# Second half's products of ones moved ahead of the first tile's products, its root ahead of a weight join, and two chunk pairs' loads held until that root is made

## The chip, the cores and the metric

The kernel runs on one core of one Trainium2 chip. The metric is the device time in microseconds of one execution, lower is better. The kernel before takes 598.52 us in the median of three runs.

## What is computed

Three stages follow each other on 4 x 768 = 3072 tokens of 256 numbers: a chunked linear recurrence with decay (8 heads, 32 wide, state 16), a gated network of width 1536 behind an RMS norm, and a second gated network of width 2048. All of it is float32.

```python
def _attn_ref(x, a, B, C):
    ...
    for c in range(nc):
        ...
        L = np.exp(cum[:, :, :, None] - cum[:, :, None, :]) * causal
        CB = np.einsum('bhin,bhjn->bhij', Cc, Bc)
        y_intra = np.einsum('bhij,bhjd->bhid', CB * L, xc)
        y_inter = np.einsum('bhin,bhnd->bhid', Cc, state) * decay_to_i[:, :, :, None]
        ...
        state = decay_full[:, :, None, None] * state + np.sum(Bx, axis=2)

def _moe_ref(x, w_gate, w_val, w_out, rms_g):
    rms = np.sqrt(np.mean(x * x, axis=-1, keepdims=True) + 1e-06)
    xn = x / rms * rms_g
    g = xn @ w_gate
    silu = g * (1.0 / (1.0 + np.exp(-g)))
    return silu * (xn @ w_val) @ w_out

def _moe2_ref(x, w_in, w_out):
    h = x @ w_in
    g = h * np.clip(h + 3.0, 0.0, 6.0) / 6.0
    return g @ w_out
```

## The kernel before

**Work items.** The recurrence works on 24 chunks (number k), two at a time: a pair of chunks has the number q = k // 2. Chunks 0 to 3 (pairs 0 and 1) belong to the first 128 positions of the four batches; their 512 tokens are the first token tile (j = 0) of the first network. Pairs 2 and 3 are the next 512 tokens, and so on. The network's weights come as 12 tiles f = 0 to 11 of 768 columns; each tile is loaded by SyncE's queue (`yT<-w`, `rawx<-w`), converted by ScalarE (`wa`, `wb`: lines 831 and 835), joined by VectorE (`wj`, line 839), and split into a high part (`wh`, a CAST at line 292 or 294) and a low part (`wl`, a TENSOR_TENSOR at line 288), which are both called `w1t` in the profile. A product of the network is three passes: high x high, low x high, high x low.

**Order.** `P.op` records each operation with an estimated cost, what it reads and writes; `Plan.run` places them on the engines in the order of a simulated schedule, and `P.chain` fixes the order of named operations on one engine by hand. So the order is decided when the program is built; on the chip each engine runs its list in order and waits on semaphores. The schedule of GpSimd (POOL) holds the DMAs of the chunk pairs from pair 2 on: `L` (the decays, spread over 64 partitions), `cb` (B, C and x of the pair) and `P` (the decay products).

**The opening.** For the first tile the norm is done in two halves of two chunks (`norm_pair`, q = 0 and 1). For the second half, the steps are:

- `sq2`, `sq3` (ScalarE, line 637): squares of the recurrence's output; `mn2`, `mn3` (TensorE, line 658): products with a column of ones, which sum them;
- `rt1` (ScalarE, line 695): square root; `v1`, `iv1`, `nw1` (VectorE, lines 691, 699, 678 to 680): mean, reciprocal, one Newton step;
- `bk1` (TensorE, line 703): spreads the factor; `sx10`, `sx11` (VectorE, line 708): scale x; `xh10`, `xh11` (ScalarE) and `xl1` (VectorE): split x into high and low.

The first products of the network, `h000`, `h001`, `h100`, `h101` (weight tile, half, gate or value), use the first half; `h010` and those after it use the second half. Between the visit `visit1` and `h010` the plan puts idle products of zeros (`idle`, line 389, about 0.43 us each, written to `acc` or `sps`) where it sees TensorE waiting. Behind `h010` the plan's own order goes on: the products of tiles f = 2, 3, ..., the visits of the chunk pairs, the norm of the next token tile.

The calls for the second half's loads stand at line 495 and after (`ld_L`, `ld_cb2`, `ld_P`); a weight load that writes the same buffers as an earlier one waits for its readers. Chunk pair 2 and pair 3 each load two `L` of 256 KB, a `cb` of 896 KB and two `P` of 64 KB.

Of the kernel before, what the change touches and what calls it, by code (L numbers as in the profile page):

```python
# [16 lines left out]
B, H, S, D, N = 4, 8, 768, 32, 16  # L17
CH = 128
SC = 64
# [200 lines left out]
def block_kernel(ctx, tc, comb, ablk, a1st, w1, w2d, cst, out):  # L220
    nc = tc.nc
    pe, act, dve, pool = nc.tensor, nc.scalar, nc.vector, nc.gpsimd
# [32 lines left out]
    P = Plan({"L": 2, "cb": 2, "P": 2, "ch": 4, "bh": 2, "SM": 4, "um": 4, "V": 6, "V1": 4,  # L255
              "Sc": 1, "Su": 1, "Sy": 1, "Ss": 1, "xT": 1, "sq": 1, "rn": 1, "rb": 1, "x": 2, "p": 3, "gh": 3,
              "gl": 3, "raw": NRAW, "tmp": 3, "raw2": 1, "s2": 2, "st": 1, "h": 2, "hb": 4, "acc": 2})
# [7 lines left out]
    def dma(nbytes, n=1, e="DMA"):  # L265
        return {e: max(560 * n, nbytes // 370) if e == "DMA" else (1000 if e == "POOL" else 560) * n,
                "bytes": nbytes}
# [54 lines left out]
    pref = dram.tile([NK, H * CH], F32, name="pref")  # L322
# [57 lines left out]
    def tile2(n, q, shape):  # L380
        if (n + "2", q) not in T:
            t = T[n + "2", q] = ap2.tile([128, 2] + shape, F32, tag=n, name=n)
            for i in range(2):
                T[n, 2 * q + i] = t[:, i]
        return T[n + "2", q]
# [60 lines left out]
    def load(q):  # L446
        k0, bst = 2 * q, BOOST if 2 * q >= B else BOOST0
# [21 lines left out]
                pool.dma_start(out=t[:, i], in_=src.to_broadcast([H, N, CH]))  # L469

        cbs, Ls = [("cb", q, i) for i in range(2)], [("L", q, i) for i in range(2)]
        seq = [("raw", 3)] if q == B // 2 else []
        if q == 0:
            P.op(dma(8192, 1, "ACT"), lambda e: act.dma_start(
                out=ac[:32, 4], in_=a1st),
                w=[("ac", 1)], boost=2e6)
            P.op(dma(400000), lambda e: nc.sync.dma_start(out=ac[:, :4], in_=rows(ablk)),
                 w=[("ac", 0)], boost=1e6)
            P.op(dma(33792, 1, "ACT"), lambda e: act.dma_start(out=gs, in_=cst), w=[("cs", 0)],
                 boost=75e4)  # L480
            P.op({"ACT": 1500}, lambda e: act.activation(out=spare, in_=half, func=AF.Sqrt),
                 w=[("table", 0)], boost=5e5)
            prefixes()
            broadcast()
        if q < B // 2:
            for i, e in enumerate(("ACT", "DMA")):
                P.op(dma(458752, 1, e), lambda e, i=i: ld_cb(e, i), w=[cbs[i]],
                     boost=8e5 - 1e5 * q)
        if q == B:
            def hold(e):  # L490
                t = tile2("L", q, [H, SC])
                pool.tensor_copy(t[:, 0, 0, :1], T["sq", 1][:, 0, NT // NB - 1:NT // NB])

            P.op({"POOL": 200}, hold, r=[("sq", 1, B - 1)], w=Ls, boost=bst)
        if q >= B // 2:
            P.op(dma(1048576, 2, "POOL"), ld_L, r=[("azero", 0)], w=Ls, boost=bst, seq=seq)
            P.op(dma(917504, 1, "POOL"), ld_cb2, w=cbs, boost=bst, seq=seq)
            P.op(dma(262144, 2, "POOL"), ld_P, r=[("pref", 0), ("pref", 1)], w=[("P", q)], boost=bst)


        def scan(e, k):
# [16 lines left out]
        for i, k in enumerate((k0, k0 + 1)):  # L518
            P.op({"DVE": ds(512)}, lambda e, k=k: scan(e, k),
                 r=[("eye8", 0), Ls[i] if k >= B else ("Lp", k)], w=[Ls[i]], boost=bst,  # L520
                 seq=[("x", 0, 1, 2)] if q == B // 2 else [], tag=f"scan{k}")
# [3 lines left out]
                 w=[("ch", k)], boost=bst, tag=f"ch{k}")  # L525
# [55 lines left out]
    def back_keys(k):  # L581
        r = [("SM", k), ("cb", k // 2, k % 2), ("V1", k), ("ch", k)]
        return r + ([("V", k - B)] if k >= B else []), [("Sy", k // 2, k % 2)]
# [77 lines left out]
    def rn(j):  # L661
        if ("rn", j) not in T:
            T["rn", j] = [ap1.tile([128, B], F32, tag=n, name=n) for n in ("v0", "y0", "z0")]
        return T["rn", j]
# [177 lines left out]
    def weights(f, cols, src, raw, tmp, wh, wl, bst=0, soon=0, seq=(), hold=()):  # L842
# [28 lines left out]
        if hold:  # L871
            P.op({"POOL": 200}, lambda e: hold[0](raw(f)), r=hold[1], w=[kr], boost=soon, seq=seq)
        P.op(dma(size), load, w=[kr], boost=soon, seq=seq)
        if wide:
            P.op({"ACT": a1(cols)}, high, r=[kr], w=[kt], boost=bst, tag=f"wa{f}")
# [152 lines left out]
    def first(ks):  # L1028
        intra(ks)
        inter(ks, 1)  # L1030

    load(0)
    for q in range(2):
        ks = [2 * q, 2 * q + 1]
        for k in ks:
            rf, wf = front_keys(k)
            P.op({"PE": 350}, lambda e, k=k: score(k), r=rf[:1] + [("open0", 0)][:q], w=wf[:1],
                 boost=BOOST0 + 3000, ps=q, tag=f"sc{k}")
        for k in ks:
            rf, wf = front_keys(k)  # L1040
            P.op({"PE": 250}, lambda e, k=k: grow(k), r=rf, w=wf[1:], boost=BOOST0 + 3000,
                 seq=[("Sc", q, 1)], ps=q, tag=f"gr{k}")
        if q == 0:
            spread[0]()
            load(1)
            P.op({"HOST": 0}, open0, r=[("L", n, i) for n in range(2) for i in range(2)] +
                 [("P", n) for n in range(2)] + [("z", 0)], w=[("open0", 0)])
    for q in range(2):
        ks, r, w = [2 * q, 2 * q + 1], [], []
        for k in ks:  # L1050
            middle(k)
            r, w = r + back_keys(k)[0], w + back_keys(k)[1]
# [4 lines left out]
         w=[("open", 1)])  # L1057
    P.op({"ACT": 1500}, lambda e: act.activation(out=spare, in_=half, func=AF.Silu),
         r=[("rn", 0, q, 2) for q in range(2)], w=[("table", 0)], boost=1e6,
# [4 lines left out]
    def hold(f):  # L1064
        def go(t):
            pool.tensor_copy(t[:, :1], T["cb", 3][:, :1])

        return (go, [("cb", 1, 1)]) if f == 3 else ()

    for f in range(F1):  # L1070
        weights(f, 768, w1, raw1,
                lambda f: yflat[:, 4608 + f % 3 * 768:][:, :768] if f % 3 < 2 else extra, w1h, w1l,
                bst=(W0 - 2000 * f if f < 2 else 0), soon=1e5 if f < 2 else 0,
                seq=[("azero", 0)] + ([("raw", 3)] if f > 3 else []), hold=hold(f))
# [35 lines left out]
    for j in range(NJ):  # L1110
        acc = [nxt(nacc), nxt(nacc)]
        for f in range(F1):
# [14 lines left out]
            if n == NB - 1:  # L1127
                P.op({"HOST": 0}, open2, r=[("yT", i, t) for i in range(NJ * B, NK) for t in range(2)],
                     w=[("open", 2), ("open", 0)] + [("un", n) for n in range(NU)])
# [334 lines left out]
    while pending:  # L1464
# [1 line left out]
        pending.pop(0)[1]()  # L1466
    P.chain("PE", order)
    P.chain("DVE", "spot0 spot1 spot2 spot3 clip each prefix scan0 bh0 scan1 bh1 ch0 ch1 SM0 SM1 um0 "
            "um1 scan2 scan3 bh2 bh3 ch2 ch3 wj0 v0 iv0 nw0 SM2 SM3 um2 um3 sx00 sx01 wl0 xl0 wj1 wj2 "
            "v1 iv1 nw1 wl1 sx10 sx11 xl1")  # L1470
    P.chain("ACT", "P0 P1 wa0 wb0 sq0 sq1 wa1 rt0 ev0 ev1 wh0 wb1 wa2 xh00 xh01 sq2 sq3 wb2 wh1 rt1 ev2 "
            "ev3 silu xh10 xh11")
    P.chain("PE", "heat sp0 sp1 sc0 sc1 px gr0 gr1 sp2 sp3 visit0 zero mn0 mn1 sc2 sc3 gr2 gr3 bk0 warm visit1 "
            "h000 mn2 mn3 h001 bk1 h100 h101")
    P.fill = idle, 430, "visit1", "h010"
    with tc.manual_schedule():
        setup()
# [59 lines left out]
```

## Time and profile before

| what | us or share |
|---|---|
| median of three runs (lowest, highest) | 598.52 (597.91, 599.05) |
| profiled execution | 598.91 |
| its span in the trace | 596.8 |
| TensorE busy, share of the span | 587.6, 98% |
| VectorE busy | 475.2, 80% |
| ScalarE busy | 369.3, 62% |
| GpSimd busy | 34.9, 6% |
| DMA issues: `w` tiles of 768 KB (page, 6) | 4.7 to 10.4 us to landing |
| instruction queue q8 (page, 3) | 34 packets, 0.56 MB |

The profiled execution lies 0.39 us above the median. Of its 598.91 us, 2.1 lie outside the span. A busy time is a sum over the whole span, in which the stages have different limits. The granted TensorE clock is at its upper level (2.4 GHz) from 5.7 us on, the whole stretch that this text speaks of.

### The profile page before, as it was taken

The page shows a single profiled execution, that of the slowest core. Times are in us where ns is not written, and L with a number is a line of the kernel's source. Part 1 is how long each engine was busy: PE and PEld are TensorE (multiplying, and loading weights), DVE is VectorE, ACT ScalarE, POOL GpSimd, SP SyncE. Part 2 cuts the span into 40 slices and gives each one's busy share as a digit, 9 for nine tenths or more (in the row PEclk, how much of TensorE's full clock was granted, in tenths as well). Part 3 has the DMA queues.
Part 4 walks back from the last instruction along what each step waited for, and adds up shares of the span by engine and source line. Part 5 has one row for each costly group of instructions (what it writes and reads, how often), then busy time and mean ns, then how long its engine had stood idle before and what let it go on. Part 6 is the DMA issues. An engine that isn't in the chain of part 4 may idle for free.

```text
span 596.8 us, 10877 instructions
## 1 busy us (share of the span) xinstructions
PE 587.6 (98%) x4356; PEld 474.8 (80%) x4356; DVE 475.2 (80%) x911; ACT 369.3 (62%) x649; POOL 34.9 (6%) x63
## 2 busy tenths in 40 slices
PE   9899999999999999999999999999999999999997
PEld 6787888788778778877787878888888888888885
DVE  8899977947886588799998898887975759765665
ACT  3889523333433354676766788787876758776663
POOL 3202013102220000000000000000000000000000
PEclk9999999999999999999999999999999999999999
DMA  8994205304340010122010102100000000100001
GB/s 332 340 322 151 65 18 153 115 11 125 123 154 20 22 68 23 49 71 70 1 70 2 70 2 70 71 1 1 36 36 1 0 2 0 72 0 1 0 1 71
DMA packets 11131, 40.91 MB, mean 69 GB/s; under 512 B 2484, under 2 KB 3208, under 8 KB 10056
## 3 DMA queue, kind: packets, MB, share of 16 engines
q1 hardware_dynamic: 6312, 23.25, 10.9%
q0 software_dynamic: 4000, 15.74, 8.5%
q10 hardware_dynamic: 768, 1.22, 0.6%
q8 instruction: 34, 0.56, 0.4%
q14 instruction: 17, 0.14, 0.1%
HBM read 36.84 MB, written 3.35 MB: 67 GB/s over the span
## 4 chain that ended last, share of the span: by engine, by line
PE 89%; DVE 7%; ACT 1%; issue 1%; DMA 1%; DVEq 0%; ACTq 0%; SPq 0%
PE hps L917 59%; PE acc L917 24%; PE sps L562 1%; DVE st L288 1%; DVE unit L288 1%; PE sps L536 1%; PE sps L572 1%; DMA raw<-w 1%; DVE gl L288 1%; PE spread L396 1%; PE sps L547 1%; DVE p L288 1%; DVE w1t L288 0%; DVE L L505 0%; PE acc L389 0%
## 5 line engine op out<-in xcount | busy, mean ns | idle before, releaser
L917 PE MATMUL hps<-xh,w1t 128*128 128x512 f32 (+1 forms) x544 | 146.2, 387 | 1.0 <-ACT p L946 0.8
L917 PEld LDWEIGHTS hps<-xh,w1t 128*128 128x128 f32 x544 | 99.5, 188 | 23.2 <-ACT p L946 1.3
L917 PE MATMUL hps<-xl,w1t 128*128 128x512 f32 (+1 forms) x380 | 108.8, 385 | 0.0
L917 PE MATMUL hps<-unit,w1t 128*128 128x512 f32 x324 | 90.2, 389 | 0.0
L917 PE MATMUL acc<-gh,w1t 128*128 128x512 f32 (+1 forms) x288 | 88.0, 387 | 0.0
L917 PEld LDWEIGHTS hps<-xl,w1t 128*128 128x128 f32 x380 | 70.8, 188 | 14.5
L917 PEld LDWEIGHTS hps<-unit,w1t 128*128 128x128 f32 x324 | 60.8, 188 | 12.7
L288 DVE TENSOR_TENSOR gl<-p,gh 128x512 fp32r<-128x512 f32 (+1 forms) x86 | 57.5, 674 | 14.2 <-ACT gh L954 8.0
L917 PEld LDWEIGHTS acc<-gh,w1t 128*128 128x128 f32 x288 | 53.0, 188 | 11.3 <-issue 0.6
L954 ACT CAST gh<-p 128x512 fp32r<-128x512 f32 (+1 forms) x50 | 30.2, 606 | 50.7 <-PE acc L917 50.0
L917 PE MATMUL acc<-gl,w1t 128*128 128x512 f32 (+1 forms) x158 | 60.7, 384 | 0.0
L1261 ACT ACTIVATE p<-hps,half 128x512 f32<-128x512 f32 x48 | 33.0, 688 | 34.1 <-PE hps L917 34.1
L288 DVE TENSOR_TENSOR unit<-hps,unit 128x512 f32<-128x512 f32 x36 | 24.8, 689 | 36.3 <-PE hps L917 36.2
L950 DVE TENSOR_TENSOR p<-p,hps 128x512 f32<-128x512 f32 (+1 forms) x50 | 33.1, 663 | 24.8 <-PE hps L917 21.7
L946 ACT ACTIVATE p<-hps 128x512 f32<-128x512 f32 (+1 forms) x50 | 28.9, 581 | 37.1 <-DVE gl L288 19.2
L917 PE MATMUL acc<-unit,w1t 128*128 128x512 f32 x142 | 42.8, 389 | 0.0
L1264 DVE SCALAR_TENSOR_TENSOR p<-p,hps 128x512 f32<-128x512 f32 x48 | 33.0, 687 | 10.7 <-ACT p L1261 10.5
L1261 ACT ACTIVATE p<-unit,half 128x512 f32<-128x512 f32 x48 | 34.7, 722 | 1.1 <-DVE unit L288 0.7
L1268 ACT CAST unit<-p 128x512 fp32r<-128x512 f32 x48 | 29.7, 621 | 8.9 <-DVE p L1264 7.4
L917 PEld LDWEIGHTS acc<-gl,w1t 128*128 128x128 f32 x158 | 29.7, 188 | 6.2
L1268 ACT CAST gh<-p 128x512 fp32r<-128x512 f32 x48 | 29.5, 619 | 7.2 <-DVE p L1264 6.4
L1264 DVE SCALAR_TENSOR_TENSOR p<-p,unit 128x512 f32<-128x512 f32 x48 | 33.1, 689 | 0.8 <-ACT p L1261 0.4
(181 smaller groups left out, 967.2 us busy)
## 6 DMA issues: line engine op xcount, KB each, us to landing
cb<-comb POOLq DMA_DIRECT2D x10, 896.0 KB, 5.1
raw<-w SPq DMA_DIRECT2D x8, 1024.0 KB, 4.7
L<-azero POOLq DMA_DIRECT2D x20, 256.0 KB, 4.1
yT<-w SPq DMA_DIRECT2D x6, 768.0 KB, 9.9
rawx<-w SPq DMA_DIRECT2D x6, 768.0 KB, 10.4
out<-yT SPq DMA_DIRECT2D x10, 256.0 KB, 2.1
P<-pref POOLq DMA_DIRECT2D x20, 64.0 KB, 2.5
rb<-rnd SPq DMA_DIRECT2D x5, 256.0 KB, 3.0
```

Of the source, the lines that this page charges most:

```text
L288: eng[e].tensor_tensor(out=out, in0=a, in1=b, op=op)
L396: pe.matmul(out=Q[3][:, :128 * n], lhsT=nc.const_aps.tensor(0.0, [128, 128]), rhs=nc.const_aps.tensor(0.0, [128, 128 * n]), start=True, st ...
L536: pe.matmul(out=o[64 * c:64 * c + 64, p ^ c], lhsT=cb[r, BN + c * SC:BN + (c + 1) * SC], rhs=cb[r, CP + c * CH:CP + (c + 1) * CH], start=T ...
L547: m = pe.matmul(out=o[32 * p:32 * p + 32, c], lhsT=b[r, s:s + 32], rhs=cb[r, XX + 64 * p:XX + 64 * p + 64], start=False, stop=True, skip_g ...
L562: pe.matmul(out=part(k, Y)[32 * g:32 * g + 32, 2 * t + c], rhs=T["SM", k][r, h ^ 2 * c], lhsT=T["cb", k][r, XX + D * h:XX + D * h + D], st ...
L917: pe.matmul(out=o, lhsT=a, rhs=c, start=first and i == 0, stop=last and i == len(seq) - 1, skip_group_check=skip)
L946: act.activation(out=p[:, :n], in_=hcols(0), func=AF.Silu)
L950: dve.tensor_tensor(out=p, in0=p, in1=hcols(1), op=ALU.mult)
L954: act.copy(out=t[:, :n], in_=T["p", i][:, :n])
L1261: act.activation(out=unit(pk), in_=h(), func=AF.Relu, scale=1.0 / 6.0, bias=half)
L1264: dve.scalar_tensor_tensor(out=unit(pk), in0=unit(pk), scalar=1.0, in1=h(), op0=ALU.min, op1=ALU.mult)
L1268: P.op({"ACT": a1(512) + 20}, lambda e: act.copy(out=unit(gk), in_=unit(pk)), r=[pk], w=[gk])
```

## The change

Three things are edited. In the hand-written chains, TensorE now has `mn2 mn3` ahead of `h000` and `bk1` ahead of `h001`; ScalarE has `rt1 ev2 ev3` ahead of `wh1`; VectorE has `v1 iv1 nw1` ahead of `wj2`, and `wl1` behind `sx10 sx11`. GpSimd copies one column of `y` (the second half's factor) into the `L` tile of pair 2 ahead of that pair's loads, so that they cannot start before the factor is there; `cb` and `P` of the pair are ordered behind this copy, and pair 3's loads behind pair 2's `L`. The plan then makes a new order of what follows.

```diff
-        seq = [("raw", 3)] if q == B // 2 else []
+        seq = [("raw", 3)] if q == B // 2 else [("L", 2, 0)] if q == 3 else []
...
+        if q == B // 2:
+            def hold(e):
+                t = tile2("L", q, [H, SC])
+                pool.tensor_copy(t[:, 0, 0, :1], rn(0)[1][:, 2:3])
+
+            P.op({"POOL": 200}, hold, r=[("rn", 0, 1, 1)], w=Ls + [("hold", 0)], boost=bst, seq=seq)
+            seq = [("hold", 0)]
         if q >= B // 2:
             P.op(dma(1048576, 2, "POOL"), ld_L, r=[("azero", 0)], w=Ls, boost=bst, seq=seq)
             P.op(dma(917504, 1, "POOL"), ld_cb2, w=cbs, boost=bst, seq=seq)
-            P.op(dma(262144, 2, "POOL"), ld_P, r=[("pref", 0), ("pref", 1)], w=[("P", q)], boost=bst)
+            P.op(dma(262144, 2, "POOL"), ld_P, r=[("pref", 0), ("pref", 1)], w=[("P", q)], boost=bst, seq=seq)
...
     P.chain("DVE", "spot0 spot1 spot2 spot3 clip each prefix scan0 bh0 scan1 bh1 ch0 ch1 SM0 SM1 um0 "
-            "um1 scan2 scan3 bh2 bh3 ch2 ch3 wj0 v0 iv0 nw0 SM2 SM3 um2 um3 sx00 sx01 wl0 xl0 wj1 wj2 "
-            "v1 iv1 nw1 wl1 sx10 sx11 xl1")
-    P.chain("ACT", "P0 P1 wa0 wb0 sq0 sq1 wa1 rt0 ev0 ev1 wh0 wb1 wa2 xh00 xh01 sq2 sq3 wb2 wh1 rt1 ev2 "
-            "ev3 silu xh10 xh11")
+            "um1 scan2 scan3 bh2 bh3 ch2 ch3 wj0 v0 iv0 nw0 SM2 SM3 um2 um3 sx00 sx01 wl0 xl0 wj1 "
+            "v1 iv1 nw1 wj2 sx10 sx11 wl1 xl1")
+    P.chain("ACT", "P0 P1 wa0 wb0 sq0 sq1 wa1 rt0 ev0 ev1 wh0 wb1 wa2 xh00 xh01 sq2 sq3 wb2 rt1 ev2 ev3 "
+            "wh1 silu xh10 xh11")
     P.chain("PE", "heat sp0 sp1 sc0 sc1 px gr0 gr1 sp2 sp3 visit0 zero mn0 mn1 sc2 sc3 gr2 gr3 bk0 warm visit1 "
-            "h000 mn2 mn3 h001 bk1 h100 h101")
+            "mn2 mn3 h000 bk1 h001 h100 h101")
```

The new lines move the line numbers behind line 495 by 7. On TensorE, behind `visit1` (the last row of `ch,um`), the kernel before has one idle product into `sps`, two into `acc`, `h000` (six rows of `hps`), the four products of ones, `h001`, three idle products and `bk1` (`eye,y`):

```order
L572 MATMUL sps<-ch,um 64x64 x8
L389 MATMUL sps_107<-zero 128x256
L389 MATMUL acc<-zero 128x256 x2
L917 MATMUL hps<-xh,w1t_68 128x256 x4
L917 MATMUL hps<-xl,w1t_68 128x256 x2
L658 MATMUL sps<-ones,sq 128x1 x4
L917 MATMUL hps<-xh,w1t_68 128x256 x4
L917 MATMUL hps<-xl,w1t_68 128x256 x2
L389 MATMUL acc<-zero 128x256 x3
L703 MATMUL sps<-eye,y_317 128x128 x2
```

The changed kernel has at the same place:

```order
L579 MATMUL sps<-ch,um 64x64 x8
L389 MATMUL sps_107<-zero 128x256
L389 MATMUL acc<-zero 128x256
L665 MATMUL sps<-ones,sq 128x1 x4
L924 MATMUL hps<-xh,w1t_68 128x256 x4
L924 MATMUL hps<-xl,w1t_68 128x256 x2
L389 MATMUL acc<-zero 128x256 x3
L710 MATMUL sps<-eye,y_312 128x128 x2
L924 MATMUL hps<-xh,w1t_68 128x256 x4
L924 MATMUL hps<-xl,w1t_68 128x256 x2
L389 MATMUL acc<-zero 128x256 x2
```

The products of ones stand ahead of `h000`, with one idle product fewer before them; `bk1` stands ahead of `h001`; the three idle products that stood ahead of `h010` have become two ahead of `h100`. On VectorE, from the join `wj1` on, the kernel before has `wj2` (`fold`), a high part of tile 2, the second half's factor, `wl1`, `sx10 sx11`, `wl2` and `xl1`:

```order
L839 SCALAR_TENSOR_TENSOR yT<-yT 128x768
L839 SCALAR_TENSOR_TENSOR fold<-fold,yT 128x768
L294 CAST w1t_69<-fold 128x768
L691 TENSOR_SCALAR v_316<-sps 128x2
L699 RECIPROCAL y_317<-z_318 128x2
L680 SCALAR_TENSOR_TENSOR y_317<-z_318,y_317 128x2
L288 TENSOR_TENSOR w1t_68<-yT,w1t_68 128x768
L708 SCALAR_TENSOR_TENSOR xT<-xT,gs,sps 128x256 x2
L288 TENSOR_TENSOR w1t_69<-fold,w1t_69 128x768
L288 TENSOR_TENSOR xl<-xT,xh 128x2x256
```

The changed kernel has there:

```order
L846 SCALAR_TENSOR_TENSOR yT<-yT 128x768
L698 TENSOR_SCALAR v_311<-sps 128x2
L706 RECIPROCAL y_312<-z_313 128x2
L687 SCALAR_TENSOR_TENSOR y_312<-z_313,y_312 128x2
L846 SCALAR_TENSOR_TENSOR fold<-fold,yT 128x768
L294 CAST w1t_69<-fold 128x768
L715 SCALAR_TENSOR_TENSOR xT<-xT,gs,sps 128x256 x2
L288 TENSOR_TENSOR w1t_68<-yT,w1t_68 128x768
L288 TENSOR_TENSOR xl<-xT,xh 128x2x256
L957 TENSOR_TENSOR p<-p,hps 128x256
L288 TENSOR_TENSOR w1t_69<-fold,w1t_69 128x768
```

The factor stands ahead of `wj2`, `wl1` (`w1t_68`) behind `sx10 sx11`, and `wl2` (`w1t_69`) has moved behind `xl1` and the first gated product `p`. On POOL, the kernel before issues the first loads of pairs 2 and 3 in this order, behind a copy that belongs to the weights:

```order
L1066 COPY rawx_104<-cb 128x1
L454 DMA cb<-comb 128x2x896
L460 DMA L<-azero 64x1024 x2
L469 DMA P<-pref 128x1x128 x2
L460 DMA L<-azero 64x1024 x2
L454 DMA cb<-comb 128x2x896
L469 DMA P<-pref 128x1x128 x2
```

The changed kernel issues them in this one:

```order
L1073 COPY rawx_104<-cb 128x1
L498 COPY L<-y_312 128x1
L460 DMA L<-azero 64x1024 x2
L454 DMA cb<-comb 128x2x896
L469 DMA P<-pref 128x1x128 x2
L460 DMA L<-azero 64x1024 x2
L454 DMA cb<-comb 128x2x896
L469 DMA P<-pref 128x1x128 x2
```

All ten stand behind the new copy, and pair 2's `cb` behind its `L`. Further down on VectorE, the scans of pair 3 (`L<-L`, some 20 rows behind the piece above) stand in the difference of the two programs so, - before and + changed:

```order
 L288 TENSOR_TENSOR gl<-p,gh 128x256
-L505 SCALAR_TENSOR_TENSOR L<-L,eye_101 128x512
 L288 TENSOR_TENSOR w1t_70<-fold,w1t_70 128x768
-L505 SCALAR_TENSOR_TENSOR L<-L,eye_101 128x512
-L593 TENSOR_TENSOR SM<-sps,L 128x512
-L600 TENSOR_TENSOR um<-sps,gs 128x128
-L593 TENSOR_TENSOR SM<-sps,L 128x512
-L600 TENSOR_TENSOR um<-sps,gs 128x128
+L512 SCALAR_TENSOR_TENSOR L<-L,eye_101 128x512 x2
```

The first of them has moved behind a low part of a weight tile. The first scan of pair 2 likewise has one gated product `p` more ahead of it.

## Rows read from the trace of the kernel before

**Rows 1.** Windows: stretch, its length, busy us (count) of PE, PEld, DVE, ACT, POOL, clock, DMA share, GB/s.
```profile
20.00:29.00 9.00, 8.03 (x53) 7.29 (x53) 7.34 (x17) 7.18 (x15) 1.51 (x3) 1.00 1.03 296
29.00:57.70 28.70, 28.70 (x458) 23.78 (x459) 28.38 (x52) 24.88 (x42) 4.11 (x7) 1.00 0.71 236
69.60:590.00 520.40, 518.09 (x3447) 420.09 (x3446) 408.11 (x767) 318.19 (x560) 20.91 (x34) 1.00 0.13 42
```
**Rows 2.** Timeline of PE: start, us, line, operation, tiles, count [idle before <-releaser].
```profile
20.01 1.13 PE L389 MATMUL acc<-zero 128*128 128x256 f32 x4
20.79 0.83 PE L917 MATMUL hps<-xh,w1t 128*128 128x256 f32 x4
...
21.69 0.39 PE L658 MATMUL sps<-ones,sq 128*128 128x1 f32 x3
22.92 0.61 PE L658 MATMUL sps<-ones,sq 128*128 128x1 f32 x5 [0.84 <-issue]
23.39 0.72 PE L917 MATMUL hps<-xh,w1t 128*128 128x256 f32 x4
...
24.19 1.46 PE L389 MATMUL acc<-zero 128*128 128x256 f32 x6
25.48 0.61 PE L703 MATMUL sps<-eye,y 128*128 128x128 f32 x4
```
**Rows 3.** Timeline of DVE, 20 to 29 us.
```profile
20.58 0.95 DVE L839 SCALAR_TENSOR_TENSOR yT<-yT 128x768 int32<-128x768 int32 x1
...
23.86 0.16 DVE L691 TENSOR_SCALAR v<-sps 128x2 f32<-128x2 f32 x1 [0.86 <-ACT z L695]
...
24.60 0.95 DVE L288 TENSOR_TENSOR w1t<-yT,w1t 128x768 fp32r<-128x768 f32 x1
26.20 0.87 DVE L708 SCALAR_TENSOR_TENSOR xT<-xT,gs,sps 128x256 f32<-128x256 f32 x2 [0.66 <-PE sps L703]
27.00 0.95 DVE L288 TENSOR_TENSOR w1t<-fold,w1t 128x768 fp32r<-128x768 f32 x1
27.87 0.68 DVE L288 TENSOR_TENSOR xl<-xT,xh 128x512 fp32r<-128x512 f32 x1
```
**Rows 4.** Timeline of ACT, 21 to 28 us.
```profile
21.57 0.83 ACT L292 CAST w1t<-yT 128x768 fp32r<-128x768 f32 x1 [0.56 <-DVE yT L839]
23.57 0.26 ACT L695 ACTIVATE z<-sps,eps 128x2 f32<-128x2 f32 x1 [1.16 <-PE sps L658]
...
26.72 0.80 ACT L292 CAST xh<-xT 128x256 fp32r<-128x256 f32 x2
```
**Rows 5.** Timeline of DVE, 30 to 58 us.
```profile
30.67 1.22 DVE L505 TENSOR_TENSOR_SCAN L<-L,eye 128x512 f32<-128x512 f32 x1
...
39.34 1.22 DVE L505 TENSOR_TENSOR_SCAN L<-L,eye 128x512 f32<-128x512 f32 x1
40.48 0.93 DVE L288 TENSOR_TENSOR w1t<-fold,w1t 128x768 fp32r<-128x768 f32 x1
...
44.24 0.29 DVE L288 TENSOR_TENSOR bh<-cb,L 128x128 f32<-128x128 f32 x1
...
55.38 0.69 DVE L950 TENSOR_TENSOR p<-p,hps 128x512 f32<-128x512 f32 x1 [0.32 <-ACT w1t L292]
```
**Rows 6.** Timeline of POOL: the later hold of the kernel before.
```profile
54.50 0.60 POOL L492 COPY L<-sq 128x1 f32<-128x1 f32 x1
```
**Rows 7.** DMA queues from 23 to 27 us: packets, MB, share of 16 engines.
```profile
q1 hardware_dynamic: 140, 0.76, 68.4%
q0 software_dynamic: 140, 0.35, 35.9%
```
**Rows 8.** The same from 17.5 to 20 us, the POOL queue, while a cb moves.
```profile
q0 software_dynamic: 88, 0.63, 60.6%
```
**Rows 9.** DMA issue at 47.98 us: KB, us to landing.
```profile
cb<-comb POOLq DMA_DIRECT2D x1, 896.0 KB, 4.9
```
**Rows 10.** Tile L, four loads issued from 13.6 to 18.5 us.
```profile
DMA to landing us min/median/max: 12.2/14.5/16.5
```

## The prediction

> **What bounds the kernel now.** The windows come first [rows 1]. From 69.6 to 590 us TensorE is busy 518.09 of 520.40 us: nothing there waits, and the edits do not reach it. From 29 to 57.7 us TensorE is busy all 28.70 us, and VectorE 28.38 of them: two full engines, of which VectorE has a single idle of 0.32 us (at 55.38, behind a high part of a weight tile) [rows 5]. Only from 20 to 29 us is there room: TensorE 8.03 of 9.00 us, and part of that is idle products of zeros; VectorE 7.34. In the same window the DMA engines show a busy share of 1.03: every transfer there delays another.
>
> Then the timelines, engine by engine. On TensorE, `h000` starts at 20.79 and lasts 0.90, the products of ones start at 21.69, stand still for 0.84 us in the middle of the row (behind nothing that the profile shows), and are through at 23.39 [rows 2]. ScalarE, done with `wh1`, waits 1.16 us for them and takes the root at 23.57 [rows 4]; VectorE idles 0.86 us for the root, does the factor from 23.86 to 24.60, then `wl1`, idles 0.66 for `bk1`, and starts `sx10` at 26.20, `wl2` at 27.00, `xl1` at 27.87 [rows 3]. `h010` needs `xl1`, and idle products (two right ahead of `h000`, three right ahead of `bk1`) fill TensorE's gaps until then. So the second half's factor is a chain of waits worth about 1.5 us of VectorE's idle time, but VectorE, not TensorE, carries the debt afterwards.
>
> What reaches the end? Behind 57.7 us comes the next token tile's norm, a chain that VectorE begins, and behind it TensorE's full stretch from 69.6 [rows 1]. With VectorE 99% busy up to that norm, I count the gain that lasts by VectorE's shift, not by TensorE's.
>
> **The early part, term by term.** TensorE: one idle product fewer (1.29 us for three, from 24.19 to 25.48, is 0.43 each [rows 2]), so the ones start at 20.01 + 0.43 = 20.44 in place of 21.69. Without the stall the row takes 23.39 - 21.69 - 0.84 = 0.86: through at 21.30. Before, the root started 0.18 behind that end and the first step of the factor 0.29 behind the root's start [rows 2 to 4]: root 21.48, factor 21.77 to 22.51. TensorE: `h000` until 21.30 + 0.90 = 22.20, three idle products until 23.49, `bk1`; `sx10` came 0.72 behind `bk1`: 24.21, 1.99 earlier. VectorE is free for it: from 22.51 `wj2` 0.95 [rows 3] and the CAST (at most the 0.83 of ScalarE's CAST of that size [rows 4]) end by 24.29. Then `sx10 sx11` 0.80, `wl1` 0.87 (the distance to the next start), so `xl1` could go at 25.96. ScalarE ends later: root 21.48, then 3.15 to `xh10` (the distance from 23.57 to 26.72), plus `wh1` 0.83, which now stands behind the root, and 0.80 for `xh10` and `xh11` [rows 4]: 26.26. So `xl1` starts at 26.3 instead of 27.87: 1.6 earlier for `h010` and TensorE.
>
> VectorE's own account is smaller: `wl2` (0.87), done ahead of `xl1` before, is now behind the first `p`. The shift on VectorE is 1.57 - 0.87 = **0.70 us**. Two idle products fewer on TensorE cost nothing, since they only fill.
>
> Whether the 0.84 stall goes is not shown by any row. No semaphore ends it. It stands inside eight products of one form, beside DMA engines at a share of 1.03, and what TensorE has to be given there is its instructions. If it is that, it hangs on the DMA load at that time, and the hold takes POOL's 3 MB away from exactly there; I take it as gone. If it stays, 0.84 is lost from both accounts: 0.73 on TensorE, 0.14 lost on VectorE. The Trainium skill ("Runtime: NRT & Kernel Launch", section "Instruction fetch mechanics") says that engines refetch their program in blocks of 256 instructions and that a crossing is mostly hidden. By that, the stall would not be a fetch and would stay; the row, 0.84 us idle with no releaser [rows 2], fits an unhidden one better.
>
> **The hold, and what queues behind it.** POOL's copy waits for the factor at 22.51; it takes 0.60, as the later hold of the same form does [rows 6]: the first `L` is issued at 23.1. Before, the first `L` was issued at 13.6 and the fourth at 18.5 [rows 10], and `cb` before both. Behind the copy on POOL stand only the ten loads, all in order: two `L`, `cb`, two `P`, two `L`, `cb`, two `P`. The consumers that come first are VectorE's scans, and behind each scan stands all of VectorE's later work: high and low parts, gated products. Pair 2's first scan ran at 30.67; 0.70 earlier, and one `p` (some 0.4) more ahead of it, makes 30.4. Pair 3's first ran at 39.34; 0.70 earlier, but now behind a low part of 0.93 [rows 5], makes 39.6.
>
> When do the `L` land? In a stretch shared with weights, POOL's queue moved 0.35 MB in 4 us, 87 GB/s, while it held `L` and `P` [rows 7]; with `cb` moving it did 0.63 MB in 2.5 us, 252 GB/s [rows 8]. A `cb` alone, 4.9 us to landing [rows 9], is 3.6 us of bytes at that rate and 1.3 us of start. So first bytes at 23.1 + 1.3 = 24.4; pair 2's two `L`, 0.52 MB, take 6.0: 30.4, just in time. Up to pair 3's second `L` there are 1.05 MB of `L`, 0.92 of `cb` and 0.13 of `P`: 12.0 + 3.6 + 1.5 = 17.1 us, landing at 41.5 if every `L` moves beside weights, a wait of 1.9. The lower bound is everything at 252 GB/s, 8.3 us, 32.7, no wait anywhere. The upper bounds are the lags of before [rows 10], though a `cb` and its 3.6 us stood ahead of those: 23.1 + 12.2 = 35.3 for pair 2's, a wait of 4.9; for pair 3's, with the issues spread over 4.9 us as before, 28.0 + 16.5 = 44.5, a wait of 4.9 too. The two don't add up, since who has waited once is later at the other place. I take **1.0 us**, between none and 1.9: the weights run alone until 24.4 and should leave gaps later (the share from 29 to 57.7 is 0.71 on the mean [rows 1]), but under load a start is hardly shorter than that of the lone `cb`. Pair 3's `cb` follows its `L` within 3.6, 41.5 - 0.9 + 3.6 = 44.2 with that wait, and `bh`, at 44.24 before [rows 5], is due at 44.24 - 0.70 + 1.0 = 44.5: nothing more.
>
> The Trainium skill ("DMA: Bandwidth & Descriptors", section "Queues, rings and completion order") says that each DMA engine takes turns between its queues packet by packet. The row agrees: 140 packets of either queue in 4 us [rows 7]. By that rule the small packets of `L` get no more than half the turns as long as weights are queued, the stream lands at 41.5, the wait is 1.9 and the sum below becomes +0.9: it speaks against holding the loads.
>
> **Sum.** VectorE: -0.70 (early part) + 1.0 (wait for `L`) = +0.3, which the idle of 0.32 at 55.38 takes up: 0.0. The profiled execution stays at 598.9, which lies 0.39 above the median, so on the scale of the median 598.5. What a measurement of this kernel can tell from no change is about 0.2%, 1.2 us: the forecast is no visible difference.
>
> **Rivals.**
> 1. *The loads land later still*, with the lag of before: a wait of 2.5 to 4.9, less 0.70 and 0.32, makes +1.5 to +3.9: 600.0 to 602.4. For it: the share of 1.03, equal packet counts, the lags of 12.2 to 16.5 [rows 1, 7, 10]. Against: no `cb` is ahead of pair 2's `L` any more, and the weights will have run ahead. It decides from a wait of 2.2 on, a landing of pair 2's `L` at 32.6 or of pair 3's at 41.8.
> 2. *The loads are in time and the early gain arrives.* Without a wait VectorE keeps 0.70: 597.8, still within 0.2%. If TensorE's 1.6 lasts as well, because the debt of `wl2` goes into idle time, 598.5 - 1.2 to 1.6: 596.9 to 597.3, faster. Against: VectorE's 28.38 of 28.70, with almost no idle to pay from [rows 1].
> 3. *The stall stays with the products of ones*, so the edits to the chains do next to nothing: early part +0.14 in place of -0.70, the hold ends 0.84 later, the scans are due 0.84 later, so the same wait: 0.14 + 1.0 - 0.32 = +0.8, 599.3, at the edge of slower.
> 4. *A new stall of TensorE's instructions* while the held loads move, 0.84 again [rows 2]: taken up where VectorE is the bound, since TensorE is ahead by 1.6. It changes no number unless it is longer.
>
> **Chances.** The forecast (a wait of 0 to 2, VectorE's gain alone): 0.47. Rival 1: 0.25. Rival 2's faster end: 0.16. The stall that stays: 0.12, a third of it beyond 0.2%. So faster 0.16, slower 0.25 + 0.04 = 0.29, same 0.55. The range leaves at most 0.2 outside: low 597.0, inside the faster case; high 601.0, a wait of 3.5, short of the upper bounds, which need the whole lag of before although less is queued ahead.
>
> **What would show it.** In the changed kernel: ones from about 20.4 in one piece (or again with an idle behind nothing), `bk1` at 23.5, `sx10` at 24.2, `xl1` at 26.3, `h010` behind it. If `xl1` isn't ahead of 27, the early part is wrong; its likeliest failure is ScalarE, with `wh1` now behind the root. The copy on POOL near 22.5, the first `L` issued near 23.1; then the landings of the second and the fourth `L`, and VectorE's idle ahead of the scans of pairs 2 and 3, with those transfers as its end. No idle there and a time below 597.3: rival 2. An idle of 2.5 or more: rival 1. Wrong altogether I would be if a wait opened elsewhere, above all on TensorE between 29 and 57.7 us, where before there was none, or if the weights, which move alone while POOL's loads are held, had been what the opening waited for.

## The result and the profile after

| what | before | changed |
|---|---|---|
| median, five executions each (lowest, highest) | 598.66 (597.91, 599.05) | 603.12 (602.69, 603.57) |
| ratio, 95% interval | | 1.0077 (1.0065, 1.0089) |
| profiled execution, its span | 598.91, 596.8 | 603.12, 601.0 |
| TensorE, VectorE, ScalarE, GpSimd busy | 587.6, 475.2, 369.3, 34.9 | 589.1, 475.2, 369.4, 35.7 |
| mean granted clock of TensorE in the executions | 0.999 in the profiled one | 0.996 to 0.997 |

The changed kernel is 4.5 us (0.77%) slower. The forecast was no visible difference (598.5) in a range from 597.0 to 601.0; the measured time lies above it, on the side of rival 1. TensorE is busy 1.5 us longer although it has two idle products fewer. That is the first hint that something beyond a wait happened. Of the kernel before, one execution of 2048.65 us is left out in all that follows.

The windows of the changed kernel (columns as in [rows 1]):

```profile
29.00:33.40 4.40, 3.57 (x25) 2.97 (x23) 1.84 (x5) 4.11 (x9) 0.69 (x2) 1.00 1.01 241
33.40:34.90 1.50, 0.00 (x0) 0.00 (x0) 1.50 (x3) 0.65 (x1) 0.60 (x1) 1.00 1.07 287
...
36.00:37.00 1.00, 1.00 (x4) 0.71 (x3) 0.63 (x1) 0.34 (x1) 0.00 (x0) 0.50 1.05 227
37.00:38.00 1.00, 1.00 (x4) 0.81 (x3) 0.76 (x2) 1.00 (x2) 0.00 (x0) 0.50 0.96 267
38.00:39.00 1.00, 1.00 (x4) 0.79 (x3) 1.00 (x2) 0.33 (x1) 0.00 (x0) 0.50 1.09 294
...
40.00:44.00 4.00, 4.00 (x47) 3.46 (x53) 3.73 (x8) 3.50 (x7) 0.00 (x0) 1.00 1.01 316
```

Where [rows 1] showed TensorE busy all 28.70 us, it now stands still, with nothing at all from 33.4 to 34.9, and then runs at 0.50 of its clock, that is at 1.2 GHz, in every window from 36 to 39. VectorE's timeline says why (its rows answer to [rows 3, 5]):

```profile
21.86 0.16 DVE L698 TENSOR_SCALAR v<-sps 128x2 f32<-128x2 f32 x1 [0.29 <-ACT z L702]
...
25.05 0.87 DVE L715 SCALAR_TENSOR_TENSOR xT<-xT,gs,sps 128x256 f32<-128x256 f32 x2 [0.81 <-PE sps L710]
25.84 0.95 DVE L288 TENSOR_TENSOR w1t<-yT,w1t 128x768 fp32r<-128x768 f32 x1
26.71 0.68 DVE L288 TENSOR_TENSOR xl<-xT,xh 128x512 fp32r<-128x512 f32 x1
...
33.35 1.23 DVE L512 TENSOR_TENSOR_SCAN L<-L,eye 128x512 f32<-128x512 f32 x1 [2.56 <-DMA L<-azero]
...
43.60 2.33 DVE L512 TENSOR_TENSOR_SCAN L<-L,eye 128x512 f32<-128x512 f32 x2
```

The first scan of pair 2 was ready to go at 33.35 - 2.56 = 30.79 and waited 2.56 us for its `L`; pair 3's scans wait for nothing. On TensorE (answering to [rows 2]):

```profile
20.57 0.95 PE L665 MATMUL sps<-ones,sq 128*128 128x1 f32 x8
21.39 0.60 PE L924 MATMUL hps<-xh,w1t 128*128 128x256 f32 x3
22.67 0.28 PE L924 MATMUL hps<-xh,w1t 128*128 128x256 f32 x1 [0.69 <-issue]
...
24.32 0.61 PE L710 MATMUL sps<-eye,y 128*128 128x128 f32 x4
...
26.16 1.19 PE L924 MATMUL hps<-xh,w1t 128*128 128x256 f32 x4
...
28.14 0.64 PE L924 MATMUL hps<-xh,w1t 128*128 128x256 f32 x4
...
34.95 1.35 PE L924 MATMUL hps<-xh,w1t 128*128 128x512 f32 x4 [2.37 <-DVE p L957]
...
36.95 1.91 PE L924 MATMUL hps<-xh,w1t 128*128 128x512 f32 x4
...
51.48 1.20 PE L924 MATMUL hps<-xh,w1t 128*128 128x512 f32 x4
```

Behind the scan on VectorE stands a `p`, the step that reads a finished product out of its buffer and frees it for the next one. TensorE waits for that `p` and idles 2.37 us; the two sets of six products from 34.95 to 39.39 then take 4.44 us, where two sets of the kernel before take 2.72 (from 34.02 to 36.74): 1.7 us for the clock. `h010` starts at 28.14, against 28.93 before. The products behind the third visit start at 51.48; in the kernel before they started at 47.91, as its TensorE timeline shows:

```profile
47.91 1.20 PE L917 MATMUL hps<-xh,w1t 128*128 128x512 f32 x4
```

So the account to there is -0.8 (earlier `h010`) + 2.37 + 1.7 = +3.3 of the +3.57 measured (51.48 - 47.91); the 0.3 left is not traced to a row. The span's other 0.6 comes later, near 110 and 150 us, without a wait that a row shows; what it is stays open.

How the held loads went, from GpSimd's timeline and the issue of the first `L` (size, us to landing), answering to [rows 6, 10]:

```profile
22.73 0.97 POOL L498 COPY L<-y 128x1 f32<-128x1 f32 x1 [14.79 <-DVE y L687]
24.00 1.23 POOL L460 DMA_DIRECT2D L<-azero  x2 [0.30 <-POOL L L498]
...
L<-azero POOLq DMA_DIRECT2D x1, 256.0 KB, 8.2
```

and the DMA share by windows (the last two columns are DMA share and GB/s):

```profile
20.00:21.50 1.50, 1.46 (x11) 1.41 (x12) 1.50 (x3) 1.03 (x2) 0.00 (x0) 1.00 0.99 400
21.50:24.00 2.50, 1.81 (x12) 1.61 (x12) 2.06 (x8) 2.42 (x6) 0.97 (x1) 1.00 0.64 180
24.00:27.20 3.20, 3.10 (x22) 2.73 (x21) 2.40 (x5) 3.01 (x6) 3.19 (x6) 1.00 0.94 331
27.20:33.40 6.20, 5.37 (x40) 4.77 (x38) 3.64 (x9) 5.43 (x12) 2.49 (x5) 1.00 1.00 235
```

The first `L` is issued at 24.0, but the POOL queue has no packet before 27.0 and its first one between 27.0 and 27.2; then the engines are full until the scan starts. While POOL's loads were held the share fell to 0.64: time of the DMA engines that was lost, in a stretch that has none to spare.

### The profile page after: what moved, and what is told of

Same layout as the page of the kernel before. It is cut to its first block, busy times and chain, and to the rows that moved or that the text cites. A ratio compares the mean times of both kernels' runs of the same rounds, so it can differ in the third digit from the quotient of the medians.

```text
span 601.0 us, 10871 instructions
## 1 busy us (share of the span) xinstructions
PE 589.1 (98%) x4352; PEld 475.5 (79%) x4352; DVE 475.2 (79%) x911; ACT 369.4 (61%) x649; POOL 35.7 (6%) x64
## 4 chain that ended last, share of the span: by engine, by line
PE 88%; DVE 3%; ACT 1%; DMA 1%; issue 1%; ACTq 0%; DVEq 0%; SPq 0%
PE hps L924 60%; PE acc L924 24%; PE sps L569 1%; PE sps L543 1%; PE sps L579 1%; DMA rb<-rnd 1%; PE sps L554 1%; DVE unit L288 0%; PE sps L766 0%; DVE st L288 0%; DVE gl L288 0%; DVE p L1271 0%; DMA rnd<-y 0%; DVE p L957 0%; DVE raw L1163 0%
## 5 line engine op out<-in xcount | busy, mean ns | idle before, releaser
L924 PE MATMUL hps<-xh,w1t 128*128 128x512 f32 (+1 forms) x544 | 147.7, 389 | 4.0 <-DVE p L957 2.4
```

The source lines that it names most:

```text
L924: pe.matmul(out=o, lhsT=a, rhs=c, start=first and i == 0, stop=last and i == len(seq) - 1, skip_group_check=skip)
```

## The experiments

All are timed against the kernel before, whose medians in these comparisons lay between 598.50 and 598.63. "Upper clock" (for the kernel before, in each of the four comparisons) counts the executions whose mean granted clock is 0.999 or more (an average that leaves less than 2 us at half clock); "packet" is the start of the 0.2 us stretch of the profiled execution in which the 16 KB packet of the instruction queue q8 (the second of three between 9 and 30 us) was counted; "stall" is TensorE's idle behind nothing that the profile shows, at its 349th product or where that went.

| kernel | median | ratio (95%) | upper clock: count, median | packet | stall |
|---|---|---|---|---|---|
| before | 598.66 | | 23 of 23, 26 of 29, 11 of 12, 15 of 15 | 20.2 | 0.84 |
| changed | 603.12 | 1.0077 (1.0065, 1.0089) | 0 of 5 | 20.0 | 0.69 |
| copy left out | 603.09 | 1.0061 (1.0041, 1.0082) | 1 of 8, 598.86 | 22.0 | 2.34 |
| hold alone | 599.45 | 1.0018 (1.0009, 1.0028) | 10 of 11, 599.43 | 20.0 | 0.55 |
| chains alone | 600.22 | 1.0027 (1.0013, 1.0041) | 4 of 10, 598.83 | 20.0 | 0.69 |
| TensorE fed in the wait | 601.22 | 1.0046 (1.0032, 1.0060) | 6 of 6 | 19.6 | 0.41 |
| pair 2's `L` free | 600.29 | 1.0038 (1.0025, 1.0050) | 1 of 6, 600.20 | 21.6 | 2.33 |
| hold until the first factor | 599.56 | 1.0018 (1.0008, 1.0028) | 8 of 12, 598.90 | 18.8 | none |
| pair 3 held alone | 599.70 | 1.0026 (1.0011, 1.0041) | 7 of 12, 599.40 | 18.6 | none |
| place of the stall moved | 599.74 | 1.0024 (1.0015, 1.0034) | 7 of 12, 599.22 | 20.4 | not seen |
| weights held too | 605.59 | 1.0115 (1.0097, 1.0134) | 0 of 4 | 17.2 | none |
| `L` free, weights held | 601.28 | 1.0060 (1.0035, 1.0086) | 4 of 8, 600.96 | 18.2 | none |
| old chains, hold until the first factor | 599.12 | 1.0011 (1.0002, 1.0020) | 9 of 11, 599.03 | 20.6 | 0.65 |

**The copy left out.** The operation keeps its place in the plan but copies nothing, so every engine's order is that of the changed kernel.

```diff
-                pool.tensor_copy(t[:, 0, 0, :1], rn(0)[1][:, 2:3])
```

> The changed kernel with its program as it is, in the same order on every engine, but without the copy that holds the loads. Theory A (the wait for the held loads is the whole loss: 2.56 us on VectorE ahead of the first scan of pair 2, 2.37 us on TensorE behind it, and some 1.7 us in which TensorE then runs at the lower clock): the idle ahead of that scan is gone, TensorE stays at 2.4 GHz, and the time falls by 4 to 5 us to 597.8 to 599. Theory B (the new order of the products, of wl1 and wl2 and of the visits costs most of it): 601 to 603, with waits of VectorE or TensorE left between 29 and 58 us.

The wait of the scan is gone, and the time is the same. Theory A alone fails, and so does theory B, since there is no wait left between 31 and 58 us. TensorE's timeline:

```profile
21.61 0.60 PE L923 MATMUL hps<-xh,w1t 128*128 128x256 f32 x3
24.55 0.37 PE L923 MATMUL hps<-xh,w1t 128*128 128x256 f32 x1 [2.34 <-issue]
...
25.15 2.76 PE L389 MATMUL acc<-zero 128*128 128x256 f32 x6
27.70 1.06 PE L709 MATMUL sps<-eye,y 128*128 128x128 f32 x4
```

The stall stands at the same product as in the changed kernel, but lasts 2.34 us, and behind it the granted clock is 1.2 GHz (the three idle products take 2.55 us to the next start; before, 1.29 [rows 2]). One execution of eight stayed at the upper clock: 598.86.

**The hold alone**, with the old chains (the three `P.chain` lines of before).

> The kernel before with the held loads alone, old chains. The factor is made at 24.6 us there, so the loads go some 2 us later than in the changed kernel (26 in place of 24) and the scan of pair 2 is due about 1.3 us later. Theory A: an idle of VectorE of 2.5 to 4 us ahead of that scan, a stretch of TensorE at the lower clock behind it, 602.5 to 604.5 in all. Theory B: near the kernel before, 598 to 600.

```profile
DVE L L512 <- DMA L<-azero: 0.8, 1, 0.8
...
PE hps L924 <- DVE p L957: 0.5, 1, 0.5
```

Only 0.8 us of wait in these rows (us in total, times, longest) and no lower clock: theory A misses. The time, 599.45, lies where theory B put it. Two things make the wait 1.8 us shorter than in the changed kernel. The old order has the scan behind more work, so that it is due at 31.90 and not at 30.79. And the `L` is there 0.65 us earlier (the scan starts at 32.70, not at 33.35) although it is issued later, at 25.52: the POOL queue's first packet comes between 27.1 and 27.3, 1.6 us behind the issue where the changed kernel has 3.2. So the hold alone is not dear; it becomes dear with chains that want the `L` earlier, and with a slow start of the load, whose cause no run here shows.

**The chains alone** (no hold, loads issued as before).

> The edits to the chains alone; loads as in the kernel before, cb of pair 2 ahead of its L. The program on TensorE, VectorE and ScalarE is in the order of the changed kernel. Theory A: no idle ahead of the scans, TensorE at 2.4 GHz throughout, second half of the first tile 0.8 us earlier on TensorE: 597.5 to 598.8. Theory B: 601 to 603.

The median lies between the theories. Its executions, 598.21 to 601.63, differ by the clock: a median of 598.83 in the four at the upper clock, 601.02 in the six others. The profiled one is of the second kind: a stall of 0.69, then three idle products at half clock.

```profile
22.49 0.37 PE L917 MATMUL hps<-xh,w1t 128*128 128x256 f32 x1 [0.69 <-issue]
...
23.09 2.76 PE L389 MATMUL acc<-zero 128*128 128x256 f32 x6
```

**TensorE fed in the wait.**

```diff
         def hidden(e, v):
+            if b == 0 and f == NE and v == 1:
+                for _ in range(6):
+                    idle()
```

> The changed kernel with six idle products of zeros (about 0.2 to 0.4 us each) on TensorE ahead of the products that wait for the late scan, nothing else. They do no work that counts; VectorE's wait for the L of pair 2 stays at 2.4 to 2.7 us. If the lower clock behind the wait is a cost of its own, it goes away and the time falls by some 1.7 us to 601.2 to 601.8. If VectorE is what carries the delay to the end and the clock cost is hidden behind it, 602.8 to 603.4 as before.

```profile
DVE L L512 <- DMA L<-azero: 2.4, 1, 2.4
```

The wait is there, the clock does not fall (windows of this kernel):

```profile
29.00:33.00 4.00, 4.00 (x25) 3.58 (x25) 1.61 (x4) 3.71 (x8) 1.06 (x2) 1.00 1.03 294
33.00:36.00 3.00, 3.00 (x15) 2.53 (x14) 2.80 (x5) 0.58 (x2) 0.18 (x1) 1.00 1.01 211
36.00:40.00 4.00, 4.00 (x22) 3.41 (x21) 4.00 (x7) 3.27 (x6) 0.00 (x0) 1.00 1.02 302
```

601.22 is the number forecast for a cost of its own: the lower clock behind the wait is worth 603.12 - 601.22 = 1.9 us. That is a difference of medians, and the six executions lie between 599.66 and 602.17, so it is good to about 1 us; the 1.7 us read off the timeline above agrees. The profiled execution is the fastest of the six.

**Pair 2's `L` free**: the copy goes into pair 2's `cb`, behind its `L`, and holds everything else.

> The changed kernel with pair 2's two L free to move as early as before (issued near 12 us), and everything behind them (pair 2's cb and P, pair 3's loads) held until the factor; order on TensorE, VectorE and ScalarE as in the changed kernel. If the late L of pair 2 is what the change pays: no idle ahead of pair 2's scan, TensorE at the upper clock from 29 us on, the stall of TensorE after its 349th product 0.5 to 0.9 us as in the changed kernel (the POOL queue moves only 0.5 MB ahead of it), 597.5 to 599. If the stall after the 349th product grows with any load on the POOL queue: 1.5 us or more there, and 600 to 603 as without the copy.

```profile
24.12 0.28 PE L925 MATMUL hps<-xh,w1t 128*128 128x256 f32 x1 [2.33 <-issue]
```

No wait for `L`, but a stall of 2.33 us: the second case, with no more than 0.5 MB ahead of it on POOL's queue. The profiled execution stays at the upper clock all through and still takes 600.20, so a long stall costs time without the clock, too.

**Hold until the first half's factor.**

```diff
-                pool.tensor_copy(t[:, 0, 0, :1], rn(0)[1][:, 2:3])
+                pool.tensor_copy(t[:, 0, 0, :1], rn(0)[1][:, :1])
```

> The changed kernel with the same ten loads held, but only until the factor of the first half, some 7 us earlier. Order on all engines as in the changed kernel. If the late L is all that the change pays: the L land before 30 us, no idle ahead of the scans, 597.5 to 599. If the held loads are also what keeps the stall after the 349th product short: they now move while that stall is due, it lasts 1 to 2.5 us, TensorE's clock falls behind it, 600 to 603.

The median 599.56 lies between the two cases. The profiled execution has no stall and no wait, and shows the early part as it was forecast:

```profile
20.65 0.95 PE L665 MATMUL sps<-ones,sq 128*128 128x1 f32 x8
21.46 0.72 PE L924 MATMUL hps<-xh,w1t 128*128 128x256 f32 x4
...
23.55 0.61 PE L710 MATMUL sps<-eye,y 128*128 128x128 f32 x4
...
26.65 0.64 PE L924 MATMUL hps<-xh,w1t 128*128 128x256 f32 x4
```

It takes 597.79, the best of its kind; eight executions at the upper clock have a median of 598.90, the four others 600.12. Against the changed kernel, the earlier release is worth 3.6 us. The late `L` is therefore most of the loss in this order of operations, though 599.56 is still 1.1 above the kernel before (598.50 in this comparison).

**Pair 3 held alone.** The copy stands in front of pair 3's loads only.

> The changed chains with the copy in front of pair 3's loads alone, so pair 2's cb, L and P move early and pair 3's are held until the factor (the plan's order behind the first tile differs a little). Late-L theory: no idle ahead of pair 2's scans; pair 3's L land near 34 to 37, ahead of their scan at 40 or more: 597.5 to 599. Stall theory: pair 2's 1.5 MB are in the queues when TensorE reaches its 349th product: stall 0.7 to 2.3 us, 599 to 602.

The median, 599.70, lies in the range of the stall theory, but the profiled execution (598.03) has no wait for `L` and no stall at that place. The five executions with a lower clock take 600.52 to 601.97; the plan's order behind the first tile differs here, so the median tells less.

**The place of the stall moved.** On the chains alone, with four records fewer ahead of `h000` and no idle products behind it.

```diff
-NWARM = (4, 4, 1)
+NWARM = (4, 4)
...
+        nidle[0] += 1
+        if nidle[0] == 1:
+            pe.matmul(out=T["ps", 0][:, 0], lhsT=zero, rhs=four(zero), start=True, stop=True)
+        if nidle[0] < 6:
+            return
```

> The chains alone (loads as before, nothing held), with four fewer TensorE records ahead of h000: one small warming product left out, and one idle product of 512 columns in place of two of 256; the three idle products between h000 and bk1 are left out as well. In all six traces so far TensorE stands still right after its 349th matmul record, in the ones (before) or in h000 (changed). Theory: the place is fixed by the count, so that the stall now falls at the end of h000 or right behind it, ahead of bk1, and not inside it; bk1 starts within 0.3 us of the stall's end, 22.6 to 23.2, and sx10 near 23.5, 1.5 us or more ahead of the chains-only run: 597.5 to 599 in all. If the stall belongs to the products of h000 or to what they read, it stays after their third product and the time stays near 600.2.

```profile
21.27 0.72 PE L924 MATMUL hps<-xh,w1t 128*128 128x256 f32 x4
21.83 0.40 PE L924 MATMUL hps<-xl,w1t 128*128 128x256 f32 x2
23.08 0.71 PE L710 MATMUL sps<-eye,y 128*128 128x128 f32 x4 [0.85 <-ACT xT L292]
...
147.29 0.32 PE L579 MATMUL sps<-ch,V 32*64 32x64 f32 x2 [1.51 <-issue]
```

`h000` is in one piece and `bk1` starts at 23.08, as the theory of the count says; what is left of the stall can't be told from the wait for ScalarE. But the time did not follow: this execution has another stall, of 1.51 us at 147.29, and half clock behind it (601.12). It, too, ends 2.6 us behind a packet of q8, the one counted from 144.6. Such stalls can stand elsewhere.

**Weights held too**: a copy of one column of `sq3` into weight tile 4's buffer ahead of its load.

> The changed kernel with the weight loads from tile 4 on held as well, by a copy on POOL of one column of the second half's squares (ready near 19.6 us), so that the weight queue is empty from about 18 to 20.3 us. Order on all engines as in the changed kernel up to the third visit. In ten traces the stall after TensorE's 349th product ends 2.3 to 2.7 us behind a 16 KB packet of the instruction queue, which comes between 18.6 and 22.0 us. If that packet waits behind weights and pair loads in the DMA queues: it comes at 18.5 us or before, TensorE has no stall there, bk1 starts near 23.5 and xl1 near 26.3; the L then start into an emptier queue but still land after 30.5, so a wait of 1 to 2.5 us ahead of pair 2's scan stays, 600 to 602.5. If the packet comes at a time of its own: near 20.0, with a stall of 0.4 to 0.8 us, bk1 24.3, 602.5 to 603.5.

```profile
18.00:20.00 2.00, 1.93 (x83) 1.30 (x72) 2.00 (x5) 1.98 (x6) 0.00 (x0) 1.00 0.02 4
20.00:23.00 3.00, 3.00 (x22) 2.81 (x22) 2.59 (x8) 2.46 (x6) 1.85 (x2) 1.00 0.12 31
23.00:29.00 6.00, 5.90 (x45) 5.56 (x44) 5.88 (x11) 5.97 (x12) 5.47 (x9) 1.00 1.02 393
```

With the queues drained (share 0.06 from 16 to 17 us, 0.02 from 18 to 20) the packet comes at 17.2, earlier than in any kernel with full queues, and the stall is gone: as forecast for a packet that waits behind the loads. `bk1` starts at 23.21, `xl1` at 25.77. The other half of the expectation missed by far. The five empty microseconds push everything back, and the wait for `L` grows to 4.53:

```profile
34.39 1.23 DVE L512 TENSOR_TENSOR_SCAN L<-L,eye 128x512 f32<-128x512 f32 x1 [4.53 <-DMA L<-azero]
```

**`L` free, weights held.**

> Pair 2's L free to move early, all other loads of pairs 2 and 3 held until the factor, and the weight loads from tile 4 on held until the second half's squares; chains as in the changed kernel. Both causes named so far are taken away: no stall after the 349th product (packet at 18.6 us or before), no idle ahead of the scans, TensorE at the upper clock. If these two are the whole of the loss: 597 to 598.6, and no execution over 600. If the weights of tile 4 and 5 now come late: an idle behind a weight tile near 27 to 31 us and 599 to 601.

```profile
PE sps L544 <- DMA cb<-comb: 2.8, 1, 2.8
DVE L L513 <- DMA L<-azero: 2.1, 1, 2.1
```

No stall, and pair 2's scan on time. Now pair 3's `L` and its `cb` come late, in place of the weights that the expectation named: 601.28.

**Old chains, hold until the first factor.**

> The kernel before with its old chains, and the ten loads held until the factor of the first half (near 16 us); the plan moves some products of the first tile and the first visit. If the early hold alone shortens the stall after the 349th product (16 KB packet at 18.6 to 19 us in place of 20.2, so no stall inside the ones) and the old chains keep TensorE from the lower clock: root and factor 0.8 us earlier, no wait for L, 597.5 to 598.3. If a gain of that size in the opening does not reach the end, or the loads move late enough to cost as much: 598.4 to 599.5, no better than before.

```profile
23.09 0.61 PE L665 MATMUL sps<-ones,sq 128*128 128x1 f32 x5 [0.65 <-issue]
```

599.12, no better than before. In this execution the packet came at 20.6 in spite of the early hold. No version tried beats the kernel before.

## Why the prediction was wrong

Two steps decided it. The wait for `L` was put at 1.0 us and measured 2.56, because the start of the load was taken as 1.3 us and took 3.2. And what TensorE's own idle would cost in clock was put at nothing; it is worth 1.9 us. A third step, the stall taken as gone, was wrong as well. The last paragraph of the prediction named a new wait on TensorE between 29 and 57.7 us as the sign of being wrong altogether, and that is where it opened.

- **Early part.** Ones at 20.44 forecast, 20.57 measured; factor 21.77 against 21.86: right. That the stall goes with the hold was wrong. The step was "the hold takes POOL's 3 MB away from exactly there; I take it as gone". Weights alone keep the engines full until 21.5 (share 0.99), the packet came at 20.0 instead of 20.2, and the stall of 0.69 moved from the ones into `h000`. It costs `bk1` 0.83 (24.32 for 23.49). The 0.69 and the 0.84 stand at one place by count: both kernels have 349 products ahead of it (windows up to the stall, of before and of the changed kernel):

```profile
0.00:22.90 22.90, 20.07 (x349) 13.81 (x350) 20.41 (x55) 11.41 (x21) 8.66 (x20) 1.00 0.93 353
```

```profile
0.00:22.65 22.65, 19.56 (x349) 13.45 (x350) 19.52 (x58) 11.53 (x23) 3.47 (x12) 1.00 0.90 341
```

- **TensorE's 1.6 us.** 0.8 was right. `h100` reads the low part `wl1`, which now stands behind `sx10 sx11` and starts at 25.84; the row of four products of `h100` lasts 1.19 for it. `xl1` (26.71) is not the only thing that `h010` waits for. That term was mis-sized.
- **The wait for `L`.** This is the term that decided the sign: "I take **1.0 us**, between none and 1.9". Measured 2.56, at pair 2, not pair 3. Pair 2's `L` was taken as just in time, from a start of 1.3 us read off a lone `cb` [rows 9]; under load the start took 3.2 us, the copy 0.97 for 0.60, and its issue came at 24.0 for 23.1. In sum 24.4 became some 27.2 for the first bytes, and the scan started at 33.35 where 30.4 was forecast for the landing. From the first bytes to the scan it is some 6 us, as forecast for the two `L`: the start was mis-sized, while the moving took as long as forecast. The trace of before held a start under load: pair 2's `cb` was issued at 12.77 into engines at a share of 1.02, and the POOL queue's first packet came between 16.7 and 16.9, 4.0 us later. The upper bound of 4.9 held.
- **The clock, in no term and no rival.** Rival 1 with a wait of 2.56 gives 2.56 - 0.70 - 0.32 = +1.5, 600.0. The runs show 1.9 more for the clock behind the wait, and the VectorE shift of -0.70 that was to pay for part of it was not kept: the scan was due at 30.79, not 30.4. That TensorE's full 28.70 us had no slack for 2.4 us of idle stood in [rows 1]; what its own idle would cost was not asked. So rival 1 was right in the wait, but its time fell short by 3.1 us.
- **Rival 3** priced the stall at 0.84. Without the copy it lasts 2.34 and the clock falls with it; then the same chains cost as much as with the hold.
- **Two rules of the Trainium skill.** By the Trainium skill ("DMA: Bandwidth & Descriptors", section "Queues, rings and completion order") the `L` would share the turns with weights. Between 24 and 28 us the queues of the changed kernel show 23 packets of POOL's and 219 of the weights' queue, between 28 and 32 it is 174 and 18: the two hardly ran side by side there, so that stretch neither bears the rule out nor speaks against it. Where both had work the counts are equal: 140 and 140 [rows 7], and 257 and 251 between 28 and 36 us with the weights held too. What made the `L` late was its start, not its turns. The Trainium skill ("Runtime: NRT & Kernel Launch", section "Instruction fetch mechanics") has a crossing of a 16 KB block as mostly hidden; I weighed that the stall would then be no fetch and would stay. It stays, and the runs point to a fetch that is not hidden: one visible stall among the 34 packets of the kernel before, so "mostly" agrees.

So the cause as far as shown, taken in this order of comparisons: of 4.5 us, 1.9 are the clock behind the wait (fed in the wait), some 1.7 the wait (601.22 against 599.56 with the loads released earlier, where the stall of 0.41 is gone too), and some 1.0 belongs to the changed chains. Without a late `L` these give 599.6 to 600.3, and 603.09 in the one kernel whose stall grew to 2.34 and took the clock along, so the parts do not simply add up. Part of that 1.0 goes with the executions that leave the upper clock. In those that stay there, the chains give medians of 598.83 to 599.40 (the four kernels with at least four such executions and no wait), which is still 0.2 to 1.0 above the kernel before at that clock (598.63 and 598.40 in the two comparisons). The best single executions (597.79 and 598.03) are no better than the best of the kernel before (597.35). Why an opening that is 1 to 2 us shorter gives back all of its gain even then was not settled.

## What to carry to other kernels

Here a hold in a stretch where the DMA engines were full left them partly empty (a share of 0.64), and what was held landed too late. So ask first for the landing that has the least slack in the *new* order, and price its start from a start under load. Ask of each wait on a full TensorE what its clock does behind it; here an idle of 2.4 us cost 1.9 more. An idle of TensorE in the middle of equal products, with no releaser, is worth counting: if it stands behind the same number of products in two kernels, look for a packet of the instruction queue just before it. Here it was the program's own loading, as far as the runs show, and moving work across it moved that work into the stall.

## What the runs showed of the hardware that was not expected

- TensorE's stall follows a 16 KB packet of the instruction queue. With the packet at 17.2 to 18.8 us (four kernels) there is none; at 19.6 it is 0.41, at 20.0 0.55 to 0.69, at 20.2 0.84, at 20.6 0.65, at 21.6 2.33, at 22.0 2.34. In all that stall, it ends 2.3 to 2.7 us behind the packet (22.92 behind 20.2, 24.55 behind 22.0). So do the five later idles behind nothing of 0.3 us or more: 0.39 us up to 150.50 (copy left out), 0.61 up to 47.86 (hold alone), 0.39 up to 148.21 (chains alone), 0.36 up to 145.71 (pair 3 held alone) and the 1.51 up to 147.29. The queue keeps TensorE's pace: from 300 to 580 us the kernel before runs 1221 products and 1220 weight loads while ten of its packets come, 244 to a packet. Only the kernels with weights held show what moves the packet, each in one execution; why it differs between near-equal kernels stays open.
- The granted clock fell to 0.50 in or behind idles of 0.69 (chains alone), 1.51, 2.34, 2.37, 2.84 (`L` free, weights held) and 4.41 us (weights held too), and did not fall behind 0.69 in the changed kernel's opening nor behind 2.33 with pair 2's `L` free. The length of the idle alone doesn't tell it.
- The first packet of POOL's queue, idle until then, came 1.6 us behind the issue of a load (hold alone), 3.2 in the changed kernel and 4.0 in the kernel before; what sets it stays open.
- GpSimd's copy of one column (128x1) took 0.18 us at 16.68 (hold until the first factor), 0.60 in [rows 6] and 0.97 in the changed kernel.
